# Loading batch 0 in head groups, filling TensorE's early gaps, and placing every step anew in an attention and channel-mix kernel

## The chip, the cores and the metric

The kernel runs on one core of a Trainium2 chip. The metric is device time in microseconds (us) from the start to the end of one execution. The kernel before takes 203.94 us (median of three runs, 203.87 to 204.32).

A core has five engines, each with its own instruction stream that it works off in order: TensorE (PE in the profile; its weight loads are listed as PEld), VectorE (DVE), ScalarE (ACT), GpSimd (POOL) and SyncE (SP). They meet only through semaphores. Transfers between HBM and the on-chip memory are issued by one of the engines and carried out by 16 DMA engines that all queues share.

## The reference

Two layers follow each other. B = 8 batches, H = 8 heads, S = 576 positions, D = 64, M = 32 memory slots; then a channel mix with d_model = 512 and d_ff = 1024.

```python
a = softmax(phi, axis=2)                          # over the 32 slots
k_m = einsum('bhsm,bhsd->bhmd', a, k)
v_m = einsum('bhsm,bhsd->bhmd', a, v)
attn = softmax((1 / sqrt(D)) * q @ k_m.T)         # 576 x 32 per head
x = attn @ v_m                                    # heads side by side: B x S x 512
x_prev = x shifted by one position, zero first
xk = mu_k * x + (1 - mu_k) * x_prev
xr = mu_r * x + (1 - mu_r) * x_prev
k = maximum(xk @ w_k, 0)
v = k * k @ w_v
out = sigmoid(xr @ w_r) * v
```

The inputs q, k, v and phi are float32 (38 MB read from HBM together with the weights), the output is float32; matrix products run in bfloat16.

## The kernel before, in words

**Layout.** A batch has eight heads. They lie in two parity halves of 64 partitions (`ROWS`) and, along the free dimension, in four head pairs (`HH`). A transfer of k, q or v casts float32 to bfloat16 and is issued by GpSimd; phi stays float32. There are two buffers for each of k, v, q and phi, used by even and odd batches in turn, so a load for batch b+2 has to wait until batch b's readers are done. Loads wait in one queue (POOL's), in the order in which they are issued.

**Steps.** Every piece of work is a named step, and `PLAN` is a flat list of the steps in the order in which they are issued. A step issues its instructions to the engines that it uses; since every engine is in order, `PLAN` also fixes the order on each engine. There is no other scheduler. A word is `batch:step`, `cN:f` (one of 8 feature blocks of chunk N of the first mix matmul), `g:t`, `sg:p`, `o:t` (by tiles of 128 tokens), or `p:what` (a load).

The steps of a batch, with their lines before:
- `exp` (L226, ACT) exponentiates phi; `z` (L248, PE) sums it, with a reciprocal on DVE; `kv`, or `k` and `v` singly (L238, PE), contract it with k and v: 72 small matmuls per call.
- `nk`/`ak` normalise k on DVE or ACT, `tk` (L307, PE, copy L312 on DVE) transposes it; `q0`, `q1` (L325, DVE) transpose two head pairs of q each, as soon as q has landed.
- `s` (L340, PE; four exponentials L345 on ACT) makes the scores. It needs `tk` and both q steps.
- The denominator goes either over PE and ACT (`l0`..`l3` L355/L360, `h..z` or `r..z` L365, products `y` or `w` L389 on DVE) or wholly over DVE (`fe`, `fs`, `fo`, `w`: L370 to L389).
- Batches 0 and 1 multiply attention by v with mu already folded in (`nk0`..`nr1` L435, then `mk1`, `mk0`, `mr1`, `mr0`, L294/L452). Batches 2 to 7 make x (`x0`, `x1`: L294, L401 on ACT), the difference (`dd`, DVE) and the mixes (`k0d`, `k2d`, `r0d`, `r2d` on DVE; `r0e`, `r2e` with a product on ACT).

The steps of the mix: `cN:f` is four matmuls (L525), a relu on ACT (L529) and a square on DVE (L533); `g:t` is four matmuls (L548) and an exponential on ACT (L553); `sg:p` finishes the sigmoid for two tiles on ACT (L559, L560); `o:t` is eight matmuls (L574), a product on DVE (L576) and two stores from SP (L510). `a` and `b` mark halves in chunk 0 and in the first four output tiles.

All PSUM tiles come from one pool of eight.

**Batch 0.** Its k, q and v come as two transfers each of 64 partitions (`0a`, `0b`: one parity half with all four head pairs). The first half is used as soon as it is there: `k0c`, `hn0`, `ht0`, `qh0`, `s0` work on one parity, `k1c`, `hn1`, `ht1`, `qh1`, `s1` on the other. `0:mub` broadcasts mu over partitions from a third and fourth small load (`mu_r`). `0:busy6` issues six matmuls of zeros whose result nobody reads. Later loads are issued partly by `p:` words and partly by `b:load`, which issues phi, k, v and q of batch b+2 together.

Of the kernel before, what the change touches and what calls it, by code (L numbers as in the profile page):

```python
# [19 lines left out]
    "0:exp1 0:mub 0:exp0 p:k:0b 0:k0c 0:z 0:hn0 0:k1c p:q:0a 0:ht0 p:q:0b 0:hn1 p:v:0b 0:qh0 0:qh1 p:v:0a 0:s0 0:l1",  # L20
    "0:ht1 0:h1z 0:l0 0:mu 0:s1 0:y1 0:v1c 0:v0c 0:nk1 p:wk:0-4 0:nr0 p:wr:0-4 p:wk:4-8 0:nk0 0:l3 0:h0z 0:y0 0:l2",
    "0:h3z 0:h2z 0:busy6 0:y3 0:y2 0:nr1 0:mr1 0:mk0 g:3 0:mk1 c0:2a 0:mr0 c0:0a p:phi:1 1:exp 7:load p:k:1 c0:4a",
    "c0:1a g:2 c0:0b c0:6a 1:z c0:5a p:q:1 c0:1b 1:k 1:nk sg:1 g:0 6:load 1:q0 1:tk 1:q1 c0:4b c0:5b g:1 c0:7b c0:2b",
    "1:s p:v:1 c0:7a c0:3b c0:3a c0:6b 1:l2 1:v 1:nk1 1:nr1 1:nk0 p:wv:0-2 1:l1 1:l3 1:nr0 1:h2z 1:h1z 1:l0 1:y2 1:y1",
    "1:h3z p:wv:2-4 0:load 1:load 1:y3 1:h0z 1:y0 o:2a o:3a 1:mk1 1:mk0 1:mr0 2:exp c1:5 c1:0 c1:7 1:mr1 c1:3 2:z",
    "c1:1 c1:4 o:3b sg:0 2:kv 2:nk o:2b 2:tk 2:q0 2:q1 c1:2 c1:6 o:1b 2:s 2:nv o:1a 3:exp 2:fe g:5 g:4 2:fs 2:fo 2:w0",
    "3:z sg:2 2:w1 o:0b o:4 o:5 2:x0 3:kv 3:nk g:7 3:nv 3:q0 2:x1 g:6 2:load 3:tk 3:q1 2:dd o:0a sg:3 2:k0d g:8 3:s",
    "4:exp 2:k2d o:6 o:7 3:l1 3:l3 3:l2 2:r0d 3:l0 c2:4 3:r0z 3:w0 3:r1z 3:w1 c2:1 c2:3 3:load c2:0 c2:7 c2:2 4:z",
    "2:r2d 3:x1 4:q0 c2:5 c2:6 3:x0 4:kv 3:dd 4:q1 4:ak 3:k2d g:9 sg:4 o:8 4:tk o:9 3:k0d 4:av 5:exp g:12 g:11 g:10",
    "5:z 4:s 3:r2d 5:kv 3:r0d 4:fe 5:q0 sg:5 c3:2 5:q1 c3:1 c3:7 4:fs 5:av c3:5 g:13 4:fo 5:load 4:load c3:6 4:w0",  # L30
    "7:exp 4:w1 5:ak c3:4 c3:3 o:10 sg:6 o:11 c3:0 7:q1 4:x1 g:14 g:15 7:z 4:x0 sg:7 7:q0 5:tk 4:dd o:12 o:15 6:exp",
    "7:kv 7:ak 5:s 7:av 4:k2d 4:k0d o:14 5:fe 7:tk 4:r2e 6:z o:13 5:fs c4:3 4:r0e 5:fo c4:4 5:w1 c4:5 6:kv 7:s 6:av",
    "6:ak 5:w0 6:q1 6:q0 c4:6 c4:1 g:19 7:fe c4:2 g:16 g:17 5:x0 c4:0 6:tk c4:7 7:fs 5:x1 sg:8 5:dd g:18 sg:9 o:17",
    "5:k0d 5:k2d 6:s o:16 o:19 o:18 5:r2e 5:r0e c5:5 6:fe c5:1 g:21 c5:2 g:20 6:fs c5:0 6:fo sg:10 6:w0 6:w1 c5:3",
    "g:23 c5:4 c5:6 g:22 c5:7 7:fo 6:x1 o:20 7:w0 7:w1 6:x0 sg:11 6:dd o:21 o:22 7:x0 g:25 6:k0d g:24 6:k2d 7:x1",
    "sg:12 7:dd o:23 7:k0d g:26 7:k2d c6:0 6:r0e c6:1 c6:4 6:r2e c6:7 c6:3 c6:5 c6:2 c6:6 c7:4 7:r0e c7:2 c7:7 c7:3",
    "g:27 7:r2e c7:6 c7:0 sg:13 c7:1 o:26 o:25 c7:5 o:27 g:29 o:24 c8:1 c8:4 g:31 g:28 c8:3 sg:14 c8:6 c8:7 g:30 c8:5",
    "o:28 o:29 sg:15 c8:2 o:30 o:31 c8:0 g:33 g:32 sg:16 g:35 g:34 o:33 o:32 sg:17 o:34 o:35",
]

LOADS = {None: ("phi", "k", "v", "q")}
PRE = "k:0a id:"
# [7 lines left out]
def kernel(  # L50
# [94 lines left out]
    def preload(word):  # L145

        what, _, part = word.partition(":")
        if what in weights:
            dst, src = weights[what]
            f0, f1 = (int(x) * 128 for x in part.split("-"))  # L150
            nc.gpsimd.dma_start(out=dst[:, :, f0:f1], in_=src[:, :, f0:f1])
        elif what == "id":
            make_identity(nc, identity)
        else:
            n = int(part[0])
            if what == "phi":
# [19 lines left out]
    sel = const.tile([HH, HH, M], F32, name="sel")  # L176
    nc.vector.tensor_copy(sel, identity[0:HH, 0:HH].unsqueeze(2).to_broadcast([HH, HH, M]))
# [14 lines left out]
    def keep_busy(n):  # L192

        ps = psum.tile([128, CT], F32, name="idle", tag="ps", bufs=8)
        for _ in range(n):
            nc.tensor.matmul(ps.rearrange("p (a b) -> p a b", b=128), lhsT=zeros, rhs=zeros.unsqueeze(1).to_broadcast([128, CT // 128, 128]), start=True, stop=True,  # L196
                             skip_group_check=True)

    def load_mu_b():
        ps = psum.tile([128, 2, 2, D], F32, name="mub", tag="ps", bufs=8)  # L200
        nc.tensor.matmul(ps.rearrange("p w c d -> p (w c d)"), lhsT=sel.rearrange("k g m -> k (g m)"),
                         rhs=mu_r.rearrange("k w c d -> k (w c d)"), start=True, stop=True,
                         skip_group_check=True)
        nc.vector.tensor_copy(mu_m[:, :, 0], ps)
        nc.vector.tensor_scalar(mu_m[:, :, 1], ps, -1.0, 1.0, op0=AL.mult, op1=AL.add)
# [6 lines left out]
    def attention(b):  # L212
# [15 lines left out]
        def ekv(parts, cs=(0, 1)):  # L228

            def go():  # L230
                w = parts.stop - parts.start
                kvps = {c: ps_tile([128, w, D], F32, "kvps") for c in cs}
                for i in range(w):
                    st.setdefault("kv"[parts.start + i], {}).update({c: kvps[c][:, i, :] for c in cs})
                for j in range(NJ):
                    for g in range(HH):
                        for c in cs:
                            nc.tensor.matmul(kvps[c][g * M:(g + 1) * M], lhsT=em[ROWS[c], j, g, :],  # L238
                                             rhs=kv5[ROWS[c], parts, g, j, :],
                                             start=j == 0, stop=j == NJ - 1,  # L240
                                             skip_group_check=True)
            return go
# [54 lines left out]
        def reload():  # L297
            if b + 2 < B:
                load_batch(b + 2)

        def tr_k(cs=(0, 1)):

            def go():
# [8 lines left out]
                nc.vector.tensor_copy(st["kmT"][rows_], ps[rows_])  # L312
# [116 lines left out]

        def norm_mu(w, c):  # L430

            def go():
                if ("vm", w) not in st:
                    st["vm", w] = work.tile([128, 2, 2, D], BF16, name="vm", tag="vm", bufs=2)
                nc.vector.scalar_tensor_tensor(  # L435
                    st["vm", w][:, :, c], in0=st["v"][c].unsqueeze(1).to_broadcast([128, 2, D]),
                    scalar=st["rz"][:, c:c + 1], in1=mu_m[:, w, :, c], op0=AL.mult, op1=AL.mult)
            return go

        def mixed(w, hf):  # L440

            def go():
# [7 lines left out]
                for i in range(ND):  # L450
# [6 lines left out]
                 "z": esum, "nk": norm_k(), "nv": norm_v(), "ak": norm_k(by_act=True), "av": norm_v(True), "tk": tr_k(), "s": scores((0, 1)), "load": reload, "mu": load_mu, "mub": load_mu_b,  # L457
                 "zr": sum_rows}
        steps.update(fe=fold_e, fs=fold_sum, fo=fold_out)
        for i in range(2):  # L460
            steps[f"q{i}"] = turn_q(slice(0, 128), slice(2 * i, 2 * i + 2))
            steps[f"qh{i}"] = turn_q(ROWS[i], slice(0, HH))
            steps[f"k{i}c"] = ekv(slice(0, 1), (i,))
            steps[f"v{i}c"] = ekv(slice(1, 2), (i,))
            steps[f"exp{i}"] = lambda i=i: exp_phi(slice(2 * i, 2 * i + 2))
            steps[f"hn{i}"] = norm_k((i,))
            steps[f"ht{i}"] = tr_k((i,))
            for w in range(2):
                steps[f"n{'kr'[w]}{i}"] = norm_mu(w, i)
# [45 lines left out]
    def keys(c):  # L515
# [3 lines left out]
        def key(fi, lo, hi):  # L519
            def go():  # L520
# [8 lines left out]
                nc.scalar.activation(rl, pk, AF.Relu)  # L529
                cut = min(hi, -(lo + 1) // (2 * S) * (-2 * S))  # L530
                for p0, p1 in ((lo, cut), (cut, hi)) if cut < hi else ((lo, hi),):
                    p = p0 % (2 * S)
                    nc.vector.tensor_mul(sq[:, fi, p:p + p1 - p0], rl[:, p0 - lo:p1 - lo], rl[:, p0 - lo:p1 - lo])  # L533
            return go

        if c == 0:
            return {f"{fi}{'ab'[hf]}": key(fi, sl.start, sl.stop) for fi in range(NF) for hf, sl in enumerate(HALVES)}
        return {str(fi): key(fi, start, end) for fi in range(NF)}
# [92 lines left out]
```

## Time and profile before

| what | value |
|---|---|
| median of the runs | 203.94 us |
| profiled execution: span from first to last instruction | 202.5 us |
| between the two, outside the span | 1.4 us |
| PE busy | 187.8 us (93%) |
| ACT busy | 156.7 us (77%) |
| DVE busy | 147.2 us (73%) |
| POOL busy | 29.3 us (14%) |
| loads through POOL's queue | 20.91 MB written on chip |
| first matmul starts | 5.90 us |
| last matmul ends | 198.8 us |

How to read it: the span is the profiled execution's own time; the runs are timed without the profiler, and the difference is what lies around the span. The second part of the page cuts the span in 40 slices of 5.06 us and gives each engine's busy share in tenths. A row of the groups has the line, the engine, what is written from what, the number of instructions, their busy time and mean length, and then the idle time in front of them with its cause. The DMA issues list the time from issue to landing.

### The profile page before, as it was taken

The page shows a single profiled execution, that of the slowest core. Times are in us where ns is not written, and L with a number is a line of the kernel's source. Part 1 is how long each engine was busy: PE and PEld are TensorE (multiplying, and loading weights), DVE is VectorE, ACT ScalarE, POOL GpSimd, SP SyncE. Part 2 cuts the span into 40 slices and gives each one's busy share as a digit, 9 for nine tenths or more (in the row PEclk, how much of TensorE's full clock was granted, in tenths as well). Part 3 has the DMA queues.
Part 4 walks back from the last instruction along what each step waited for, and adds up shares of the span by engine and source line. Part 5 has one row for each costly group of instructions (what it writes and reads, how often), then busy time and mean ns, then how long its engine had stood idle before and what let it go on. Part 6 is the DMA issues. An engine that isn't in the chain of part 4 may idle for free.

```text
span 202.5 us, 5375 instructions
## 1 busy us (share of the span) xinstructions
PE 187.8 (93%) x2167; PEld 97.2 (48%) x2167; DVE 147.2 (73%) x348; ACT 156.7 (77%) x312; POOL 29.3 (14%) x45
## 2 busy tenths in 40 slices
PE   0649899999999999999999999999999999999992
PEld 0414476646655445544456754444444444444451
DVE  2276646966898989999789979998998845243232
ACT  3135799796858989899896999988899993493670
POOL 7643222212204100036000000000000000000000
PEclk9999999999999999999999999999999999999999
DMA  6999999999999999979999300530242004404425
GB/s 154 156 206 206 267 207 201 263 221 269 224 260 251 245 305 218 276 135 206 258 247 257 95 0 3 122 85 3 55 104 53 0 3 96 112 0 104 107 63 144
DMA packets 24537, 31.29 MB, mean 155 GB/s; under 512 B 1968, under 2 KB 19648, under 8 KB 24512
## 3 DMA queue, kind: packets, MB, share of 16 engines
q0 software_dynamic: 17392, 20.91, 55.5%
q1 hardware_dynamic: 6352, 9.19, 17.4%
q10 hardware_dynamic: 768, 0.85, 1.3%
q8 instruction: 17, 0.28, 0.5%
q14 instruction: 8, 0.07, 0.1%
HBM read 38.28 MB, written 9.44 MB: 236 GB/s over the span
## 4 chain that ended last, share of the span: by engine, by line
PE 90%; DMA 4%; ACT 2%; DVE 1%; POOL 1%; issue 1%; POOLq 0%
PE pk L525 31%; PE pv L574 30%; PE pr L548 16%; DMA q<-in_q_dram 4%; PE kvps L238 3%; PE scps L340 2%; PE mxps L294 2%; PE nops L294 2%; PE zps L355 1%; PE idle L196 1%; PE zps L248 1%; DVE qT L325 1%; POOL kv L111 1%; PE ktps L307 1%; ACT lz L360 0%
## 5 line engine op out<-in xcount | busy, mean ns | idle before, releaser
L525 PE MATMUL pk<-xkT,wk 128*128 128x512 bf16 (+4 forms) x352 | 67.9, 340 | 0.0
L574 PE MATMUL pv<-wv,sq 128*128 128x512 bf16 (+1 forms) x328 | 66.4, 353 | 0.0
L529 ACT ACTIVATE rl<-pk 128x512 bf16<-128x512 f32 (+3 forms) x80 | 41.5, 566 | 13.6 <-PE pk L525 12.7
L525 PEld LDWEIGHTS <-wk 128*128 128x128 bf16 x352 | 32.9, 98 | 28.7 <-issue 0.8
L533 DVE TENSOR_TENSOR sq<-rl 128x512 bf16<-128x512 bf16 (+5 forms) x104 | 31.5, 334 | 19.4 <-ACT rl L529 18.8
L574 PEld LDWEIGHTS <-sq 128*128 128x128 bf16 x328 | 31.1, 98 | 29.7 <-issue 0.8
L548 PE MATMUL pr<-wr,xrT 128*128 128x512 bf16 x144 | 35.4, 379 | 0.8 <-ACT xkT L452 0.8
L576 DVE TENSOR_TENSOR o<-sg,pv 128x512 f32<-128x512 f32 (+1 forms) x41 | 24.5, 616 | 13.3 <-PE pv L574 13.1
L553 ACT ACTIVATE sg<-pr 128x512 f32<-128x512 f32 x36 | 21.4, 610 | 5.9 <-PE pr L548 5.1
L548 PEld LDWEIGHTS <-xrT 128*128 128x128 bf16 x144 | 13.4, 98 | 15.5 <-ACT xkT L452 1.0
L559 ACT ACTIVATE sg<-sg 128x1024 f32<-128x1024 f32 x18 | 19.4, 1079 | 0.2
L560 ACT ACTIVATE sg<-sg 128x1024 f32<-128x1024 f32 x18 | 19.0, 1058 | 0.6
L401 ACT CAST x<-nops 128x320 bf16<-128x320 f32 (+1 forms) x48 | 15.7, 424 | 3.2 <-PE nops L294 3.2
L345 ACT ACTIVATE e<-scps 128x288 bf16<-128x288 f32 x32 | 10.6, 415 | 8.3 <-PE scps L340 8.1
L325 DVE STREAM_TRANSPOSE qT<-q 128x576 uint32<-128x576 uint32 (+1 forms) x16 | 13.3, 839 | 1.2 <-DMA q<-in_q_dram 1.1
L389 DVE TENSOR_TENSOR atn<-e,lz 128x576 bf16<-128x576 bf16 (+2 forms) x20 | 12.1, 634 | 0.9 <-ACT lz L365 0.5
L424 ACT ACTIVATE mu_d<-diff,mu 128x576 bf16<-128x576 bf16 x16 | 11.6, 798 | 0.2 <-DVE xkT L427 0.2
L226 ACT ACTIVATE em<-ph 128x1152 bf16<-128x1152 f32 (+1 forms) x9 | 9.5, 1060 | 2.5 <-DMA ph<-in_phi_dram 2.5
L427 DVE TENSOR_TENSOR xrT<-x,mu_d 128x1152 bf16<-128x1152 bf16 x12 | 9.1, 755 | 3.2 <-ACT mu_d L424 3.0
L426 DVE TENSOR_SCALAR mu_d<-diff,mu 128x576 bf16<-128x576 bf16 x32 | 10.2, 363 | 0.0
L238 PE MATMUL kvps<-kv,em 64*32 64x128 bf16 (+1 forms) x720 | 8.9, 218 | 0.9 <-DMA kv<-in_k_dram 0.9
L108 POOL DMA_DIRECT2D kv<-in_k_dram x7 | 5.2, 746 | 31.3 <-PE kvps L238 26.3
(65 smaller groups left out, 148.1 us busy)
## 6 DMA issues: line engine op xcount, KB each, us to landing
out_dram<-o SPq DMA_DIRECT2D x61, 128.0 KB, 2.4
ph<-in_phi_dram POOLq DMA_DIRECT2D x7, 576.0 KB, 19.1
kv<-in_k_dram POOLq DMA_DIRECT2D x7, 576.0 KB, 18.0
q<-in_q_dram POOLq DMA_DIRECT2D x7, 576.0 KB, 19.8
kv<-in_v_dram POOLq DMA_DIRECT2D x7, 576.0 KB, 21.0
out_dram<-o SPq DMA_DIRECT2D x18, 64.0 KB, 5.9
wk<-in_moe_w_k_dram POOLq DMA_DIRECT2D x2, 512.0 KB, 15.6
wv<-in_moe_w_v_dram POOLq DMA_DIRECT2D x2, 512.0 KB, 20.6
```

The lines of the kernel that those rows point to most:

```text
L238: nc.tensor.matmul(kvps[c][g * M:(g + 1) * M], lhsT=em[ROWS[c], j, g, :], rhs=kv5[ROWS[c], parts, g, j, :], start=j == 0, stop=j == NJ - 1 ...
L325: nc.vector.transpose(dst.bitcast(U32), src.bitcast(U32))
L401: nc.scalar.copy(st["x"][:, i, sl], pss[i])
L525: nc.tensor.matmul(pk[:, p0 - lo:p1 - lo], lhsT=wk_sb[:, di, fi * 128:(fi + 1) * 128], rhs=xk_T[:, di, p0 % RING:p0 % RING + p1 - p0], sta ...
L529: nc.scalar.activation(rl, pk, AF.Relu)
L533: nc.vector.tensor_mul(sq[:, fi, p:p + p1 - p0], rl[:, p0 - lo:p1 - lo], rl[:, p0 - lo:p1 - lo])
L548: nc.tensor.matmul(pr, lhsT=xr_T[:, di, c0:c0 + 128], rhs=wr_sb[:, di, :], start=(di == 0), stop=(di == ND - 1))
L553: nc.scalar.activation(sg[:, t % 2], pr, AF.Exp, scale=-1.0)
L559: nc.scalar.activation(gated[p], gated[p], AF.Ln, bias=1.0)
L560: nc.scalar.activation(gated[p], gated[p], AF.Exp, scale=-1.0)
L574: nc.tensor.matmul(pv[:, cols], lhsT=sq[:, fi, p:p + 128], rhs=wv_sb[:, fi, cols], start=(fi == 0), stop=(fi == NF - 1))
L576: nc.vector.tensor_mul(o[:, cols], gated[t // 2][:, t % 2, cols], pv[:, cols])
```

## The change

Batch 0's transfers are cut by head pairs instead of by parity: `0g` is head pairs 0 and 1, `0h` head pairs 2 and 3, both over all 128 partitions. They are issued in the order k `g`, q `g`, k `h`, q `h`, v `g`, v `h` (before: k a, k b, q a, q b, v b, v a). `kg0`, `kg1`, `vg0`, `vg1` contract one group each into the same PSUM tiles; normalisation, transposition and q's turn then cover all 128 partitions. `nm0` and `nm1` (one for each parity) fold mu in for both mixes in one instruction each. The two `mu_r` loads go; `mub` uses `mu2`, which is loaded anyway, and two matmuls. 36 matmuls of zeros (before: six) stand in seven places ahead of `0:mk1`. 19 relus run on DVE (words with `v`) instead of ACT. `3:r0e` and `3:r2e` take a product from DVE to ACT, `7:r2d` brings one back; `nv`/`av` and `nk`/`ak` change sides in batches 2, 3 and 7. All loads are `p:` words of their own, in another order, and the whole `PLAN` is another one.

```diff
 PLAN = [
-    "0:exp1 0:mub 0:exp0 p:k:0b 0:k0c 0:z 0:hn0 0:k1c p:q:0a 0:ht0 p:q:0b 0:hn1 p:v:0b 0:qh0 0:qh1 p:v:0a 0:s0 0:l1",
-    "0:ht1 0:h1z 0:l0 0:mu 0:s1 0:y1 0:v1c 0:v0c 0:nk1 p:wk:0-4 0:nr0 p:wr:0-4 p:wk:4-8 0:nk0 0:l3 0:h0z 0:y0 0:l2",
-    "0:h3z 0:h2z 0:busy6 0:y3 0:y2 0:nr1 0:mr1 0:mk0 g:3 0:mk1 c0:2a 0:mr0 c0:0a p:phi:1 1:exp 7:load p:k:1 c0:4a",
-    "c0:1a g:2 c0:0b c0:6a 1:z c0:5a p:q:1 c0:1b 1:k 1:nk sg:1 g:0 6:load 1:q0 1:tk 1:q1 c0:4b c0:5b g:1 c0:7b c0:2b",
-    "1:s p:v:1 c0:7a c0:3b c0:3a c0:6b 1:l2 1:v 1:nk1 1:nr1 1:nk0 p:wv:0-2 1:l1 1:l3 1:nr0 1:h2z 1:h1z 1:l0 1:y2 1:y1",
-    "1:h3z p:wv:2-4 0:load 1:load 1:y3 1:h0z 1:y0 o:2a o:3a 1:mk1 1:mk0 1:mr0 2:exp c1:5 c1:0 c1:7 1:mr1 c1:3 2:z",
-    "c1:1 c1:4 o:3b sg:0 2:kv 2:nk o:2b 2:tk 2:q0 2:q1 c1:2 c1:6 o:1b 2:s 2:nv o:1a 3:exp 2:fe g:5 g:4 2:fs 2:fo 2:w0",
-    "3:z sg:2 2:w1 o:0b o:4 o:5 2:x0 3:kv 3:nk g:7 3:nv 3:q0 2:x1 g:6 2:load 3:tk 3:q1 2:dd o:0a sg:3 2:k0d g:8 3:s",
-    "4:exp 2:k2d o:6 o:7 3:l1 3:l3 3:l2 2:r0d 3:l0 c2:4 3:r0z 3:w0 3:r1z 3:w1 c2:1 c2:3 3:load c2:0 c2:7 c2:2 4:z",
-    "2:r2d 3:x1 4:q0 c2:5 c2:6 3:x0 4:kv 3:dd 4:q1 4:ak 3:k2d g:9 sg:4 o:8 4:tk o:9 3:k0d 4:av 5:exp g:12 g:11 g:10",
-    "5:z 4:s 3:r2d 5:kv 3:r0d 4:fe 5:q0 sg:5 c3:2 5:q1 c3:1 c3:7 4:fs 5:av c3:5 g:13 4:fo 5:load 4:load c3:6 4:w0",
...
-    "o:28 o:29 sg:15 c8:2 o:30 o:31 c8:0 g:33 g:32 sg:16 g:35 g:34 o:33 o:32 sg:17 o:34 o:35",
+    "0:busy17 0:exp0 p:q:0g 0:q0 0:mub 0:exp1 0:z 0:kg0 0:busy7_1 p:k:0h 0:kg1 0:busy2_2 0:nk p:q:0h 0:q1 0:tk",
+    "0:busy3_3 0:s0 p:v:0g 0:s1 0:busy2_4 0:l1 0:h1z 0:l3 0:busy2_5 p:v:0h 0:y1 0:vg1 0:h3z 0:y3 0:l0 0:l2 0:vg0",
+    "0:busy3_6 0:nm1 0:nm0 0:h2z 0:y2 0:h0z p:wk:0-4 0:y0 0:mk1 0:mk0 c0:2b 0:mr1 c0:1b p:wk:4-8 c0:5a c0:0av p:phi:1",
+    "c0:4bv c0:5bv 1:exp c0:4a c0:3a 0:mr0 1:z c0:3b c0:2a p:wr:0-4 c0:6b g:3 c0:0b c0:7av g:2 sg:1 0:mu p:k:1 1:k",
+    "1:nk p:q:1 1:q1 1:q0 g:1 g:0 1:tk c0:1av 1:s c0:7bv c0:6a 1:l0 p:wv:0-2 1:h0z o:3a 1:l3 1:l2 1:h2z 1:l1 1:y0",
+    "o:2a 1:h3z 1:y2 p:v:1 1:v 1:nk1 1:nk0 1:nr1 1:y3 1:h1z 1:y1 sg:0 o:0a p:wv:2-4 o:1a 1:mk0 p:phi:2 o:1b 2:exp",
+    "o:3b 1:mk1 1:nr0 o:2b p:v:2 p:k:2 c1:2 c1:5v 1:mr1 c1:7 c1:4 2:z 2:kv 2:nk 1:mr0 p:q:2 2:q0 c1:3 2:av 2:tk 2:q1",
+    "c1:1 c1:0 c1:6v 2:s o:0b 2:fe 2:fs 2:fo 2:w0 p:phi:3 3:exp p:v:3 p:phi:4 g:4 g:6 2:w1 g:5 3:z sg:2 o:4 o:5 4:exp",
+    "2:x1 p:k:3 3:kv 3:nk 4:z 3:av p:q:3 2:x0 3:q1 g:7 3:q0 3:tk g:8 p:k:4 2:dd 2:k0d 3:s 2:k2d sg:3 o:6 3:l0 3:l3",
+    "3:l2 2:r0d 3:l1 3:r0z 3:w0 o:7 3:r1z 3:w1 c2:4 c2:6 p:v:4 p:phi:5 c2:1 5:exp 2:r2d c2:3 c2:0 p:q:4 4:q1 4:kv",
+    "4:av 4:q0 3:x0 c2:2 c2:5 4:ak p:q:5 c2:7 5:z 3:x1 3:dd 3:k2d g:11 g:10 sg:5 4:tk 5:q0 3:k0d 5:q1 g:9 o:11 o:10",
+    "sg:4 o:8 3:r0e 4:s p:k:5 p:phi:6 p:v:5 5:kv 4:fe 4:fs 5:av 5:ak 3:r2e o:9 5:tk c3:7 6:exp c3:0 c3:3 4:fo c3:5",
+    "5:s 5:fe 4:w1 4:w0 g:13 c3:2 c3:4 g:14 5:fs c3:1 p:q:6 4:x1 c3:6 6:z 5:fo 4:x0 4:dd 4:k0d 4:k2d 5:w1 g:15 p:q:7",
+    "sg:7 g:12 sg:6 p:k:7 o:12 o:14 5:w0 p:phi:7 o:15 7:exp p:k:6 c4:5 c4:1 o:13 6:q1 7:z 6:q0 7:q0 4:r2e p:v:7 5:x1",
...
+    "c8:6v g:32 g:33 sg:16 g:28 c7:4v c8:0v sg:14 c8:7v o:28 c8:1 o:29 g:31 g:30 sg:15 o:30 o:33 o:31 g:34 g:35 sg:17",
+    "o:34 o:32 o:35",
 ]
-PRE = "k:0a id:"
+PRE = "k:0g id:"
...
-    mu_r = const.tile([HH, 2, 2, D], F32, name="mu_r")
-    for w, mu in enumerate((moe_mu_k, moe_mu_r)):
-        nc.sync.dma_start(out=mu_r[:, w], in_=mu.rearrange("(h c d) -> h c d", c=2, d=D))
...
+                if part[1:] in ("g", "h"):
+                    gs = slice(0, 2) if part[1] == "g" else slice(2, 4)
+                    nc.gpsimd.dma_start(out=dst[:, gs].rearrange("p h j d -> p h (j d)"), in_=rows(src)[:, gs])
...
-                for j in range(NJ):
-                    for g in range(HH):
+                for j in range(NJ):
+                    for g in gs:
...
+        def norm_both(c):
+            def go():
...
+                nc.vector.scalar_tensor_tensor(
+                    st["vm2"][:, :, :, c].rearrange("p w s d -> p (w s) d"),
+                    in0=st["v"][c].unsqueeze(1).to_broadcast([128, 4, D]),
+                    scalar=st["rz"][:, c:c + 1], in1=mu_m[:, :, :, c].rearrange("p w s d -> p (w s) d"),
+                    op0=AL.mult, op1=AL.mult)
...
-                nc.scalar.activation(rl, pk, AF.Relu)
+                if by_dve:
+                    nc.vector.tensor_scalar_max(rl, pk, 0.0)
+                else:
+                    nc.scalar.activation(rl, pk, AF.Relu)
```

## The prediction

> **What bounds the kernel now.** I read the slices first, to see which engine is full when.
>
> ```profile
> PE   0649899999999999999999999999999999999992
> ...
> DVE  2276646966898989999789979998998845243232
> ACT  3135799796858989899896999988899993493670
> ...
> DMA  6999999999999999979999300530242004404425
> ```
>
> From the fourth slice on TensorE is full, so the time is a front, some 180 us of TensorE work, and a tail. But the DMA row is full as well: from the second slice to the seventeenth, which ends at 86 us, and after one dip again to 111 us. The chain in order of time gives the edges:
>
> ```profile
> 3.13 7.54 DMA q<-in_q_dram
> ...
> 10.70 1.38 DVE qT L325
> ...
> 12.12 0.75 PE scps L340 x13
> ...
> 17.07 2.07 PE idle L196 x6
> 19.14 0.23 PE mxps L294 x4
> ...
> 85.57 0.83 PE kvps L238 x72
> ...
> 198.80 0.42 DVE o L576
> ```
>
> Batch 0's mixes (mxps) start at 19.1 us; from there to 198.8 TensorE is idle only 0.80 us before `g:3` (20.9) and 0.39 us at 38. The tail is one product and stores, 3.7 us.
>
> Then the loads. The issues, each asked for in its own window, give the microseconds to landing; the timeline gives the issue.
>
> ```profile
> 42.89 0.75 POOL L104 DMA_DIRECT2D ph<-in_phi_dram  x1 [2.89 <-ACT em L226]
> ...
> 61.93 0.75 POOL L108 DMA_DIRECT2D kv<-in_v_dram  x1
> ...
> 70.00 0.75 POOL L104 DMA_DIRECT2D ph<-in_phi_dram  x1 [4.79 <-ACT lz L360]
> ```
> ```profile
> ph<-in_phi_dram POOLq DMA_DIRECT2D x1, 576.0 KB, 20.0
> kv<-in_v_dram POOLq DMA_DIRECT2D x1, 576.0 KB, 21.0
> ph<-in_phi_dram POOLq DMA_DIRECT2D x1, 576.0 KB, 17.3
> ```
>
> Phi of batch 4 (phi4) lands at 62.9, v5 at 82.9, phi6 at 87.3, all about 20 us after issue: POOL issues far ahead, and a load lands when all issued before it has gone through. So up to 87 us a load's place in the queue, and not its issue, sets its landing. Batch 5's contraction `5:kv` ran at 85.50 with v5 there since 82.9: it did not wait.
>
> **The change, part by part.** The sum is made against the profiled execution (202.5 us; the median, 203.94, is 1.4 above it, taken as unchanged).
>
> *Front.* The new transfers have the old sizes, so by place the halves land as before: 7.47 (kvps waited for it), 9.00, 10.68 (the chain's 3.13 + 7.54), 12.39, 13.83, 15.39 (POOL's waits for them). The 17 idle matmuls end at 0.93 + 17 x 0.345 = 6.8 (0.345 is the mean of the six at 17.07), ahead of k `g`; at the later rows' 0.215 (`pr`, 0.86 for 4) or double that they end between 4.6 and 8.2, still covered, since k `h` comes only at 10.7. Then `kg1` 0.67 to 11.4, `nk` 0.61 to 12.0, but q `h` lands at 12.4: `q1` 0.77 and, behind it on VectorE, `tk`'s copy 0.25 make 13.4. Scores 0.25 and four exponentials 1.32: 15.0. Eight denominator steps on ScalarE, start to start 0.28 to 0.36: 2.6, with 0.3 for the first sum: 17.9. The last product 0.49: 18.4. So `0:mk1` starts at 18.5 instead of 19.1: 0.6 gained. The other 19 idle matmuls (at most 1.5 us in one place) lie in these waits. The missing `mu_r` loads and the fewer normalisations lie under the same waits: 0. `mub`'s two matmuls (1.19 cold) come before k `h`: 0.
>
> The trace shows the early matmuls at about half rate, though PEclk reads full in every slice: 0.345 against 0.215. *The Trainium skill, "TensorE: Matmul & The Clock Gate", Part 1, says that TensorE starts at half clock and is released after about 3.4 us of sustained matmuls; the early idle matmuls would then run the front's real ones at full clock. By it the scores (0.75 + 0.61 against 0.41 for both) and sums would give an estimated 1 us more, and `0:mk1` would start at 17.5.* The sum goes without that, since the loads below take either.
>
> *Gaps.* `c0:2b` waits for `mk1`'s copies (ACT 0.65, DVE 0.76 for two), with `mk0` (0.41) between: 0.4 of idle instead of 0.80. The 0.39 at 38 goes, because output halves now stand between `1:y1` and `1:mk0`. Gain 0.8 at most.
>
> *Relus.* 19 go from ScalarE (0.48 start to start for 512 columns) to VectorE. No VectorE relu is in the trace. Nearest are its copies of PSUM to bf16 (L452: 0.42 for 256, 0.48 for 320 columns); 0.60 start to start (L576) is the upper end for 512, 0.34 (a square, L533) the lower. I take 0.60: about 10 us more on VectorE, 157 of 202. Its worst pile-up: `5:fo 4:dd 4:k0d 4:k2d 5:w1`, 1.30 + 1.48 + 2 x 1.24 + 0.67 = 5.9 us; the first user, `c4:5`, comes after two `g` and three `o` = 6.9 us of TensorE. Covered by 1.0, so 0; if the cover goes, the excess falls on TensorE.
>
> *Loads, by place in the queue.* Old order from batch 3: phi3 k3 v3 q3 phi4 k4 v4 q4 phi5 k5 v5 q5 phi6; new: phi3 v3 phi4 k3 q3 k4 v4 phi5 q4 q5 k5 phi6 v5. Two places matter.
> - q3 now has phi4 before it: it lands where phi4 did, 62.9. Behind it on VectorE: two turns 0.69 + 0.77, the copy 0.2, so `3:s` starts at 64.6 (old: 64.82); `2:dd` and the mixes queue behind these. TensorE itself would be there at 64.82 - 0.6 - 0.8 + 0.2 (`4:z` comes earlier) = 63.6. It waits 1.0.
> - v5 now has q5 and phi6 before it: it lands where phi6 did, 87.3. TensorE arrives at 64.6 + 20.7 (old distance) - 0.2 + 0.9 (one `g` more ahead, 0.86) = 85.9. Everything behind `5:kv` on TensorE waits: the c3 chunks and, through them, all outputs.
>
> What stores do to v5: o:8 and o:9 went out at 83 to 85, in phi6's last stretch. There the loads' queue (q0) falls from 117.9% of the engines' time (80 to 82 us) to 77.9% (84 to 85) and 23.9% (85 to 86.5), while the stores' (q1) takes 23.3% and 69.1%. New o:11, o:10 and o:8 come at about the same time or later. One tile of stores more or less, 256 KB at the loads' rate (576 KB in 2.8 us, k1 to q1), is 1.3 us: v5 lands between 86.0 and 88.6. I take 87.0, a little below the place's own value, because the stores then rather follow. *The Trainium skill, "DMA: Bandwidth & Descriptors", Queues, rings and completion order, says that each DMA engine takes turns between its queues packet by packet; the shares just given agree with it; by it v5 lands near 86 if the new stores come late, and the time would be 203.5.*
>
> Behind `5:kv` the old order has o:10 and o:11, the new one o:9 and `g:12`: 0.86 less. Old distance from `5:kv` to the last matmul's end: 198.77 - 85.50 = 113.27. New end: 87.0 + 113.27 - 0.86 = 199.4, against 198.77: +0.6. Tail unchanged: after `sg:17` come `o:34 o:32 o:35`, 5.2 us of TensorE over 2.6 us of ScalarE, and the last store issues are the same. 203.94 + 0.6 = **204.5 us**.
>
> **The rivals.**
> - *TensorE paces it (faster).* v5 comes before TensorE asks. The deciding point: if `5:kv` starts before 87.0 - 0.6 = 86.4 the new kernel wins. With only q3 late, the end is 64.6 - 64.82 - 0.2 = -0.4: 203.5. With neither late, -0.6 - 0.8: 202.5. I take 203.1. For it: stores may come late, and the old engines' waits for k, q and phi come to only 4.5 us in all (phi 2.5, q 1.1, k 0.9). Against it: the same bytes stand before v5, and the DMA row has no dip before 86 us. *The clock gate's rule above would add its 1 us only here.*
> - *More waits than these (slower).* VectorE's pile-up outlasts its cover, or v6 is late too: v6 is now the last load. The old last one, q6, was issued at 93.88 and v6 before it landed at 93.14 + 14.7 = 107.8, so by place v6 lands at about 111, and `6:kv` is reached at 87.9 + 23.3 = 111.2. Each adds up to 1.2: 206.
> - *Nothing changes.* The wait at `5:kv` and the gains cancel: 203.9.
>
> **How the numbers follow.** Forecast (paced by v5) 0.52, its own range 203.5 to 205.9 from v5's 86.0 (where TensorE's own 85.9 is the floor) to 88.4; faster rival 0.25; more waits 0.17; cancelling 0.06. A measurement of this kernel tells about 0.2% (0.41 us) from no change. Of the forecast a third lies within 204.35, so same is 0.17 + 0.06 = 0.23; slower 0.35 + 0.17 = 0.52; faster 0.25. The range 202.6 to 206.4 takes in the faster rival's 202.5 nearly and most of the slower one's; about 2 in 10 lie outside.
>
> **What would show it.** Right: a TensorE wait of 0.5 to 2 us before kvps near 86, put down to a DMA of v, and one before scps near 64, put down to VectorE's qT; mxps first at about 18.5; the DMA row full to about 111 without the dip after 86. Wrong: no TensorE gap at 86 (the faster rival), or gaps after 95 before pk, pv or kvps (more waits). The prediction falls if v5 lands before 86.4.

## The result, and the profile after

The changed kernel takes 206.08 us (median of 4 runs, 206.07 to 206.46) beside 203.91 for the kernel before: a ratio of 1.0115, with an interval of 1.0098 to 1.0132. It is slower by 2.2 us; 0.6 was forecast. The profile shown is that of the run of 206.46 us. The medians of the kernel before differ by up to 0.4 us from one chip to the next (203.53 to 203.91 below), so experiments are compared by their ratio to it on the same chip, or within one chip.

The slices of the changed kernel, as they were shown for the kernel before (40 slices, now of 5.12 us):

```profile
PE   8868999898898999999999999999999999999990
...
DVE  2147968775898999999999999979797987762330
ACT  3137869855598999999899988976899926495350
...
DMA  6999999999999999999997300060603162004334
```

TensorE is busy in the first slices now (the idle matmuls), and the DMA row has no dip before its end at about 111 us. The chain in order of time (start, length, what):

```profile
4.02 8.15 DMA q<-in_q_dram
13.72 1.32 ACT e L333 x4
...
43.44 20.67 DMA q<-in_q_dram
64.13 1.44 DVE qT L313 x2
...
87.82 1.19 ACT e L333 x4
...
194.53 5.21 PE pv L587 x32
```

The row at 43.44 is the load of q3, which lands at 43.44 + 20.67 = 64.11: it sets the chain until then. There is no row of v5 near 86, where the forecast had its gate. What TensorE waited for (us in total, times, longest):

```profile
PE kvps L230 <- DMA kv<-in_k_dram: 2.3, 3, 1.2
PE scps L328 <- DVE kmT L300: 1.2, 3, 0.6
...
PE pv L587 <- ACT sg L572: 0.6, 1, 0.6
...
PE scps L328 <- DVE qT L313: 0.4, 1, 0.4
```

By place, those behind batch 0's front are: 0.55 us ahead of `o:0a` at 37.8, 0.77 ahead of `2:kv` at 47.1 (for k2), 0.29 and 0.36 in `2:s` at 52.7 and 53.3 (for q2's turn and the copy behind it), 0.59 ahead of `3:s` at 65.2 (the same for q3). After 66 us TensorE has no idle time of 0.15 us or more up to its last matmul.

The starts of the steps, read from the timelines, for one execution each; the third column is a second profiled execution of the changed kernel, e9 below.

| us | before | after | after, e9 |
|---|---|---|---|
| first scores of batch 0 | 12.12 | 13.20 | 12.85 |
| `2:kv` | 47.49 | 47.84 | 47.42 |
| `2:s` | 51.92 | 53.01 | 52.63 |
| `3:s` | 64.82 | 65.80 | 64.71 |
| `5:kv` | 85.50 | 87.25 | 86.44 |
| last matmul ends | 198.76 | 199.74 | 198.88 |
| last store issue ends | 199.87 | 201.62 | 200.77 |
| last store packet lands | 201.10 | 202.74 | 201.88 |
| last instruction ends | 202.47 | 204.68 | 203.83 |

From `3:s` to the last matmul both kernels need the same: 133.94 us before, 133.94 after (134.17 in e9). So the last matmul is later by what `3:s` is later, 0.98 us in these two executions; e9 shows that one execution scatters by 0.9. Over more executions the difference is about the same: the last matmul ends at 198.76, 198.02 and 198.26 in the three of the old order (the kernel before, e2, e7) and at 199.74, 199.25, 199.11 and 198.88 in four of the new one (the changed kernel, e1, e5, e9), 0.9 later on average. The rest comes behind the last matmul: 3.71 us before, 4.94 after, 4.95 in e9. This 1.23 is the larger part of the loss, and it stands in two places: from the last matmul to the end of the last store issue 1.11 against 1.88, and from the last landing to the end 1.37 against 1.94 (between them the changed kernel is 0.11 shorter).

Here is the end of the kernel before in its timeline (start, length, engine, line, what):

```profile
196.55 3.16 SPq L510 DMA_DIRECT2D out_dram<-o  x4
...
197.10 1.24 DVE L576 TENSOR_TENSOR o<-sg,pv 128x512 f32<-128x512 f32 x2 [1.09 <-PE pv L574]
```

And that of the changed kernel:

```profile
196.29 1.06 ACT L573 ACTIVATE sg<-sg 128x1024 f32<-128x1024 f32 x1
...
197.38 1.34 DVE L589 TENSOR_TENSOR o<-sg,pv 128x512 f32<-128x512 f32 x2 [3.84 <-ACT sg L573]
198.09 2.65 SPq L518 DMA_DIRECT2D out_dram<-o  x4
...
198.90 0.42 DVE L589 TENSOR_TENSOR o<-sg,pv 128x256 f32<-128x256 f32 x1 [0.18 <-PE pv L587]
199.77 0.42 DVE L589 TENSOR_TENSOR o<-sg,pv 128x256 f32<-128x256 f32 x1 [0.45 <-PE pv L587]
```

Before, the products wait for TensorE. After, o:34's product waits 3.84 us for `sg:17` on ScalarE, with o:32's behind it on VectorE. Both come out together at 197.4 to 198.7, and from 198.09 on SyncE issues stores with pauses of 0.2 us at most. (This window ends at 200.5 and counts four issues; the fifth, the last of `o:35`, ran from 200.83 to 201.62, though its product was done at 200.19.)

### The profile page after: what moved, and what is told of

Same layout as the page of the kernel before. It is cut to its first block, busy times and chain, and to the rows that moved or that the text cites. A ratio compares the mean times of both kernels' runs of the same rounds, so it can differ in the third digit from the quotient of the medians.

```text
span 204.7 us, 5403 instructions
## 1 busy us (share of the span) xinstructions
PE 192.6 (94%) x2197; PEld 98.5 (48%) x2197; DVE 155.8 (76%) x362; ACT 152.3 (74%) x295; POOL 30.0 (15%) x45
## 4 chain that ended last, share of the span: by engine, by line
PE 68%; DMA 14%; ACT 10%; DVE 2%; POOL 2%; issue 1%; POOLq 0%; ACTq 0%
PE pk L533 27%; PE pv L587 23%; DMA q<-in_q_dram 14%; PE pr L561 12%; PE kvps L230 2%; ACT e L333 2%; ACT sg L572 2%; PE scps L328 1%; PE nops L286 1%; DVE qT L313 1%; ACT sg L573 1%; PE mxps L286 1%; ACT lz L353 1%; ACT sg L566 1%; POOL kv L148 1%
## 5 line engine op out<-in xcount | busy, mean ns | idle before, releaser
L540 ACT ACTIVATE rl<-pk 128x512 bf16<-128x512 f32 (+3 forms) x61 | 33.8, 570 | 13.8 <-PE pk L533 13.0
L561 PE MATMUL pr<-wr,xrT 128*128 128x512 bf16 x144 | 34.9, 379 | 0.0
L589 DVE TENSOR_TENSOR o<-sg,pv 128x512 f32<-128x512 f32 (+1 forms) x41 | 24.6, 617 | 13.4 <-ACT sg L573 9.6
L313 DVE STREAM_TRANSPOSE qT<-q 128x576 uint32<-128x576 uint32 x16 | 11.9, 763 | 7.8 <-DMA q<-in_q_dram 7.8
L389 ACT CAST x<-nops 128x256 bf16<-128x256 f32 (+1 forms) x48 | 15.8, 435 | 0.9 <-PE nops L286 0.9
L538 DVE TENSOR_SCALAR rl<-pk 128x512 bf16<-128x512 f32 (+3 forms) x19 | 11.3, 594 | 2.5 <-PE pk L533 2.4
L412 ACT ACTIVATE mu_d<-diff,mu 128x576 bf16<-128x576 bf16 x18 | 13.0, 780 | 0.0
L184 PE MATMUL idle<-zeros 128*128 128x512 bf16 x36 | 10.4, 426 | 1.0 <-DVE zeros L115 1.0
L401 DVE TENSOR_TENSOR diff<-x 128x1024 bf16<-128x1024 bf16 (+1 forms) x18 | 8.9, 552 | 2.2 <-ACT x L389 2.2
L230 PE MATMUL kvps<-kv,em 64*32 64x128 bf16 (+1 forms) x720 | 8.2, 210 | 2.3 <-DMA kv<-in_k_dram 2.3
```

The costliest lines, as they stand in the source:

```text
L313: nc.vector.transpose(dst.bitcast(U32), src.bitcast(U32))
L389: nc.scalar.copy(st["x"][:, i, sl], pss[i])
L561: nc.tensor.matmul(pr, lhsT=xr_T[:, di, c0:c0 + 128], rhs=wr_sb[:, di, :], start=(di == 0), stop=(di == ND - 1))
L589: nc.vector.tensor_mul(o[:, cols], gated[t // 2][:, t % 2, cols], pv[:, cols])
```

## The experiments

In these diffs only the words that differ are shown.

**The order of the last outputs, both ways (e1, e2).**

```diff
 changed kernel, e1
-g:34 g:35 sg:17 o:34 o:32 o:35
+g:34 g:35 sg:17 o:32 o:34 o:35
 kernel before, e2
-g:35 g:34 o:33 o:32 sg:17 o:34 o:35
+g:35 g:34 o:33 sg:17 o:34 o:32 o:35
```

> The changed kernel with o:32 and o:34 exchanged at the end, nothing else. Theory A (the order of the last outputs lengthens the tail: o:34's product waits for sg:17 on ScalarE until 197.4, o:32's product stands behind it on VectorE, and both tiles' stores then stand on SyncE ahead of o:35's): the last TensorE matmul stays at 199.7, the last stores are issued about 1.2 us earlier, the tail goes from 5.0 back to 3.7 us, and the time from 206.1 to 204.8. Rival B (the tail is longer for another reason, the stores' own transfers, or ScalarE's late end): the tail stays at 5.0 us and the time at 206.1.

> The kernel before with o:32 moved behind sg:17 and o:34, as the changed kernel has it, nothing else. Theory A: the tail grows by about as much as in the changed kernel, 1.0 to 1.3 us, so 203.9 becomes 204.9 to 205.2. Rival B: the order alone costs nothing, 203.9.

Measured: e1 205.44 us, ratio 1.0094 (1.0076 to 1.0111); e2 204.26 us, ratio 1.0030 (1.0015 to 1.0044); the kernel before 203.70 on this chip. In e1 the last issue ends 1.12 us behind the last matmul, in e2 1.88: the two values of the table, exchanged. The timeline of e1:

```profile
195.82 0.69 DVE L589 TENSOR_TENSOR o<-sg,pv 128x512 f32<-128x512 f32 x1 [2.77 <-PE pv L587]
196.53 3.67 SPq L518 DMA_DIRECT2D out_dram<-o  x5
197.60 1.24 DVE L589 TENSOR_TENSOR o<-sg,pv 128x512 f32<-128x512 f32 x2 [1.09 <-PE pv L587]
```

o:32's product no longer stands behind the wait, and its stores are away before o:35's. Theory A is right in kind, at half the size: the order is worth 0.6 us (0.56 in e2's median), not 1.2. e2's interval is clear of 1; e1's overlaps that of the changed kernel, and there the trace shows the gain: its tail is 4.32 us, beside 4.94. What is left lies behind the last landing (1.99 us in e1, 1.31 in e2), where neither theory had looked.

**The exit (e5).** The trace shows POOL last: in the changed kernel its drain stands 0.44 us behind the instruction ahead of it and takes 0.24; in the kernel before 0.08 and 0.09. Nothing of the program differs there. The transfers of instructions (q14) do. The queues from 200 us on (packets, MB, share), kernel before:

```profile
q10 hardware_dynamic: 169, 0.13, 7.5%
q1 hardware_dynamic: 150, 0.12, 6.5%
```

Changed kernel:

```profile
q1 hardware_dynamic: 322, 0.39, 21.8%
q10 hardware_dynamic: 220, 0.22, 13.4%
q14 instruction: 1, 0.01, 0.3%
```

In the kernel before the last 8 KB on q14 came at 152.7 us; in the changed one they start at 204.7, in the exit. They come too late to be what POOL waited for at 203.5, but they suggest that a block of instructions ends there. POOL has 73 instructions against 79: the loads wait in other places. e5 adds four behind the last load:

```diff
     for _, _, _, step in sorted(todo, key=lambda t: t[0]):
         step()
+    filler = const.tile([1, 4], F32, name="filler")
+    for i in range(4):
+        nc.gpsimd.memset(filler[:, i:i + 1], 0.0)
```

> The changed kernel with four one-element memsets on POOL behind its last load, where POOL has nothing else to do. In the trace of the changed kernel the exit, from the last store's landing to the end, is 1.94 us against 1.37 in the kernel before: POOL, with six instructions fewer than before, stands 0.44 us ahead of its drain, and the last 8 KB of instructions come only at 204.7 us, where the kernel before had them at 152.7. Theory F (the exit is longer because POOL's last instructions are fetched late, which depends on how many instructions POOL has): with four more the drain follows at once, and 206.1 becomes 205.5. Rival G (the exit's length has another cause, such as which engine ends last): 206.1 or a little above.

Measured: 205.28 us, ratio 1.0098 (1.0076 to 1.0121). The drain follows after 0.08 us and takes 0.09; from the last landing to the end it is 1.43 us. So theory F holds for where the time goes, 0.5 us, and for the number of instructions on POOL as its cause: with four instructions more and no other change the exit is short again. The ratio alone, 0.0017 below the changed kernel's, is within its interval; the place in the trace is what shows it. In every kernel here the exit is slow where the last 8 KB come in the exit, and short where they come by 161 us. That a fetch is what POOL waits for is argued from this, not shown.

**The loads (e3, e6).** e3 takes phi4 out of q3's way:

```diff
-p:v:3 p:phi:4 g:4 g:6 2:w1 g:5 3:z sg:2 o:4 o:5 4:exp 2:x1 p:k:3 3:kv 3:nk 4:z 3:av p:q:3
+p:v:3 g:4 g:6 2:w1 g:5 3:z sg:2 o:4 o:5 2:x1 p:k:3 3:kv 3:nk 3:av p:q:3 p:phi:4
...
-3:s
+3:s 4:exp
...
-4:q1
+4:z 4:q1
```

> The changed kernel with phi of batch 4 loaded behind q of batch 3, and its exponentials and their sum (4:exp, 4:z) put behind 3:s, where the kernel before had them. Theory C (the place of q3 in the load queue still sets TensorE's start of 3:s, its last wait): q3 lands about 2 us earlier, the wait of 0.58 us ahead of 3:s goes, 4:z's 0.38 us moves behind it, and with TensorE full from there on the end comes 0.6 us earlier: 205.5. Rival D (the wait is taken up later, or VectorE's and ScalarE's queue holds 3:s just as long): 206.1; and if ScalarE then waits for phi4 at 63 us, up to 1 us more, 207.

Measured: 208.20 us, ratio 1.0231 (1.0212 to 1.0249). q3 landed at 62.1, beside 64.1 in the profile of the result and 63.0 in e9. Its first turn came at 63.16 (e9: 63.04), and `3:s` started at 64.81 without a wait (e9: 64.71). But then ScalarE had the exponentials in its fullest stretch. The timeline of e3:

```profile
74.00 1.17 ACT L216 ACTIVATE em<-ph 128x1152 bf16<-128x1152 f32 x1
...
75.70 0.33 PE L286 MATMUL nops<-atn,vb 32*64 32x320 bf16 x5 [0.75 <-ACT rl L540]
...
77.68 1.95 PE L533 MATMUL pk<-xkT,wk 128*128 128x512 bf16 x8 [0.46 <-DVE rz L243]
```

`5:kv` came at 89.22, and 2 us were lost. This is rival D, at twice its price. The early phi4 does delay q3, but it also lets `4:exp` run ahead of the crowd; the gate cannot be taken away by this exchange. e6 moves v5 alone:

```diff
-p:q:5 c2:7 5:z 3:x1 3:dd 3:k2d g:11 g:10 sg:5 4:tk 5:q0 3:k0d 5:q1 g:9 o:11 o:10 sg:4 o:8 3:r0e 4:s p:k:5 p:phi:6 p:v:5 5:kv
+p:v:5 p:q:5 c2:7 5:z 3:x1 3:dd 3:k2d g:11 g:10 sg:5 4:tk 5:q0 3:k0d 5:q1 g:9 o:11 o:10 sg:4 o:8 3:r0e 4:s p:k:5 p:phi:6 5:kv
```

> The changed kernel with v of batch 5 loaded ahead of q of batch 5, nothing else. The forecast's gate (v5 holds 5:kv at about 87): v5 lands near 79, 5:kv starts when TensorE gets there, 86.2 to 86.8, and the time falls by 0.4 to 1.0 us, to 205.1 to 205.7. Rival H (TensorE gets there at 87.2 anyway, as in the profiled execution of the changed kernel, so v5 is no gate): 206.1; if q5 or phi6, now two places later, hold ScalarE or VectorE, up to 1 us more.

Measured: 205.66 us, ratio 1.0110 (1.0087 to 1.0133). v5 landed at 79.7 (issue plus the profile's time to landing), beside 86.9 in the profile of the result and 86.3 in e9, and nothing waits at `5:kv`:

```profile
85.57 0.48 PE L328 MATMUL scps<-qT,kmT 32*32 32x288 bf16 x32
85.98 0.84 PE L230 MATMUL kvps<-kv,em 64*32 64x128 bf16 x72
```

The last matmul ended at 198.60, in an execution whose batch 0 was 0.5 us late; e5 on the same chip, with the old place of v5, ended at 199.11. The times tell no gain apart from none; e11 below says 0.1. So v5 is a gate of little height: TensorE comes to it within 0.1 to 0.7 us of its landing. e4 shows the gate itself.

**VectorE's relus (e4).**

```diff
-c0:0av c0:4bv c0:5bv c0:7av c0:1av c0:7bv c1:5v c1:6v c5:4v c6:1v c7:1v c7:5v c7:6v c7:4v c8:4v c8:5v c8:6v c8:0v c8:7v
+c0:0a c0:4b c0:5b c0:7a c0:1a c0:7b c1:5 c1:6 c5:4 c6:1 c7:1 c7:5 c7:6 c7:4 c8:4 c8:5 c8:6 c8:0 c8:7
```

> The changed kernel with its 19 VectorE relus back on ScalarE, nothing else. If the relus on VectorE cost nothing (TensorE has no idle time after 66 us, and the three relus before that lie beside other work), the time stays at 206.1 or rises, as ScalarE gets some 10 us more work: 206.0 to 207.0. Rival E (VectorE's 11 us more work delay q's turns and the products, so the relus are part of the loss): 205.0 to 205.6.

Measured: 206.17 us, ratio 1.0132 (1.0113 to 1.0151): the time stays. VectorE fell from 155.8 to 145.6 us busy and ScalarE rose from 152.3 to 160.3, and neither counts. In this execution TensorE was a little earlier, and the timeline shows what the forecast had described:

```profile
85.76 0.48 PE L327 MATMUL scps<-qT,kmT 32*32 32x288 bf16 x32
86.98 0.80 PE L229 MATMUL kvps<-kv,em 64*32 64x128 bf16 x72 [0.74 <-DMA kv<-in_v_dram]
```

The same wait for v5 stands in e1 (0.17 us, `5:kv` at 86.83), e5 (0.36, 86.81) and e9 (0.20, 86.44).

**The idle matmuls (e7, e8, e10).** e7 puts the front block into the kernel before; e8 takes all 36 out of the changed one; e10 cuts them to 128 columns and puts all in front, so that the number of instructions stays.

```diff
 kernel before, e7
-0:exp1 0:mub
+0:busy17 0:exp1 0:mub
 changed kernel, e8
-0:busy17 0:busy7_1 0:busy2_2 0:busy3_3 0:busy2_4 0:busy2_5 0:busy3_6
 changed kernel, e10: as e8, and
+0:busy36x1
```

> The kernel before with the 17 idle matmuls put in front, nothing else: the part alone. If the early idle matmuls release TensorE's clock (full at 3.8 us in the changed kernel, at 18.5 us before) and this shortens the front's scores and sums, batch 0's mixes start 0.3 to 1.0 us earlier and the time falls to 203.0 to 203.6. Rival I (the front is paced by loads, VectorE and ScalarE, or the loads of batches 2 and 3 take the gain back): 203.9.

> The changed kernel without its 36 idle matmuls, nothing else. If the clock's early release matters, the first matmuls run at half rate, batch 0's mixes start 0.5 to 1.5 us later, and the time is 206.5 to 207.5. If the front's waits cover them, or the load gates at 47, 53, 65 and 87 us take the difference: 206.1, and no later start of 5:kv than 87.3.

> The changed kernel with its 36 idle matmuls cut to 128 columns and all put in front, none left between the waits; the number of TensorE's instructions is the same. In e8 TensorE stood 1.65 us at 113 us with nothing to wait for, while a block of its instructions was being fetched. Theory J (that stall came from the moved instruction stream, and the idle matmuls themselves are worth nothing, because TensorE waits for v5 at 86.9 with or without them): no stall at 113, 5:kv at 86.8 to 87.3, the same time as the control within 0.4 us. Rival K (the idle matmuls between the waits are worth the 1.9 us that e8 lost): 1.5 to 2 us above the control.

Measured: e7 203.43 us beside 203.53, ratio 0.9998 (0.9985 to 1.0010): nothing, rival I. The windows of e7 (us, TensorE busy, granted clock, DMA share, GB/s) show one reason:

```profile
5.00:10.00 5.00, 4.59 (x94) 1.00 1.19 190
10.00:15.00 5.00, 2.40 (x37) 0.50 1.20 200
15.00:20.00 5.00, 5.00 (x120) 0.50 1.25 208
20.00:25.00 5.00, 4.89 (x85) 0.97 1.16 265
```

The clock is granted in full at 6.63 us, taken back at 10.05 and granted again at 20.29; in the kernel before it came at 18.5. (The view reads 1.00 ahead of the first grant too, but the idle matmuls come 0.43 us apart up to 6.63 and 0.21 behind it.) At 10.05 TensorE had stood for only 0.2 us of its wait of 1.9 us for batch 0's scores, so the length of that wait is not what took the clock. In the 3.41 us before 10.05 TensorE was busy for 87%, while the changed kernel kept the clock over such a stretch of 60% (7.25 to 10.67 us), with seven idle matmuls in it. What decides is not shown by these runs. What they show is that seventeen matmuls in front did not hold the clock in the kernel before, and that the changed kernel, with 19 more in its later waits, held it from 3.84 to 201.8 us.

e8: 207.82 us, ratio 1.0206 (1.0182 to 1.0230), 1.8 above the changed kernel by the ratios. But it was not late by 87 us: `5:kv` started at 86.90. The loss comes at 113 us:

```profile
111.60 1.54 PE L229 MATMUL kvps<-kv,em 64*32 64x128 bf16 x135
...
114.78 0.28 PE L229 MATMUL kvps<-kv,em 64*32 64x128 bf16 x9 [1.65 <-issue]
```

In the middle of 144 short matmuls TensorE stands 1.65 us and waits for nothing that the profile shows; a transfer of 16 KB of instructions ran from 112.1 to 113.3. That TensorE stood for these instructions is argued from the times, not shown. e10 has no such stall, at 206.63 us, ratio 1.0152 (1.0120 to 1.0184), against 205.97 for e9 on the same chip. Its windows:

```profile
5.00:10.00 5.00, 1.36 (x49) 0.79 1.14 169
10.00:15.00 5.00, 2.18 (x71) 0.50 1.22 207
15.00:20.00 5.00, 2.72 (x83) 0.50 1.20 257
20.00:25.00 5.00, 4.97 (x63) 0.50 1.22 216
```

Here the clock was full from 4.5 to 7.9 us and then at half until 25.0, and `2:kv` started at 50.0 instead of 47.4; by `5:kv`, 87.97 against 86.44, some of that was made up. Theory J is right on the stall: with the instructions' number kept it is gone. On the worth of the fillers it is not settled: 0.7 us by the medians, but e10's runs spread from 205.72 to 207.31 and the two intervals overlap.

**The control and the three edits together (e9, e11).** e9 is the changed kernel again; e11 has the edits of e1, e5 and e6.

> The changed kernel as it is, as the control beside the next two, and a second profiled execution of it. Ratio to the kernel before 1.010 to 1.013; 5:kv at 86.8 to 87.3, waiting for v5 where TensorE comes before 86.8; tail about 5.0 us with the slow exit of 1.9.

> The changed kernel with the three edits together: o:32 ahead of o:34, four memsets on POOL at its end, v5 loaded ahead of q5. If the three are separate costs, they add: 0.6 + 0.57 + 0.2 to 0.5, so 1.4 to 1.7 us below the control, 0.7 to 0.9 above the kernel before on the same chip, or less if batch 0's mixes are not late as in e6; the tail is 3.7 us, as in the kernel before. If they share a cause, less than 1 us below the control.

Measured on one chip: the kernel before 203.62, e9 205.97, ratio 1.0120 (1.0093 to 1.0147), e11 204.82, ratio 1.0058 (1.0037 to 1.0080). The tail of e11 is 3.84 us, near the 3.71 of the kernel before. `5:kv` came at 86.44 in e9, a little ahead of the 86.8 to 87.3 expected. The intervals of e9 and e11 do not overlap. 1.15 us are won, 1.11 of it in the tail by the traces; v5's part is 0.1 (`5:kv` at 86.35), so my sum of 1.4 to 1.7 was too high by that term. 1.2 us stay, nearly all ahead of the last matmul. None of the versions is faster than the kernel before; e11 is the fastest of the complete changed ones.

**The stores (e12).** e12 leaves out the stores of the first four output tiles, so it does not write these outputs.

```diff
-            eng.dma_start(out=dst, in_=o[p:p + n, cols])
+            if t > 3:
+                eng.dma_start(out=dst, in_=o[p:p + n, cols])
```

> The changed kernel with the stores of tiles 0 to 3 (batch 0's outputs, 1 MB) left out, so these outputs are not written; all else as it is. In the changed kernel the stores moved 855 KB between 40 and 52 us against 273 KB in the kernel before, and k2 and q2 landed 0.8 and 1.4 us later. Theory L (early stores slow the loads, and these hold 2:kv, 2:s and 3:s): k2 lands by 46.5 and q2 by 49.2, the waits of 0.5 to 0.8 us ahead of 2:kv and of 0.7 in 2:s go, 3:s starts at 64.0 or earlier, and v5 lands earlier too; the time falls by 0.6 to 1.2 us, to a ratio of 1.006 to 1.009. Rival M (the loads' bytes alone set the landings): the waits stay, ratio 1.011 to 1.013.

The queues from 40 to 52 us (packets, MB, share of 16 engines), q0 the loads' and q1 the stores'. Before:

```profile
q0 software_dynamic: 1926, 2.58, 108.9%
q1 hardware_dynamic: 331, 0.27, 9.1%
```

After:

```profile
q0 software_dynamic: 1594, 2.18, 90.0%
q1 hardware_dynamic: 1046, 0.85, 27.4%
```

e12:

```profile
q0 software_dynamic: 2029, 2.93, 117.5%
```

The load of q3 as the issues list it (issued at 43.24), in e12:

```profile
q<-in_q_dram POOLq DMA_DIRECT2D x1, 576.0 KB, 16.7
```

Measured: 204.21 us, ratio 1.0025 (1.0011 to 1.0039). By issue plus time to landing, k2 lands at 45.8 instead of 47.7, q2 at 48.7 instead of 51.6, q3 at 60.0 instead of 64.1 (63.0 in e9); the waits at 47, 53 and 65 us are gone, `3:s` starts at 62.95 and `5:kv`, without a wait, at 84.46. The timeline at `2:kv`, changed kernel:

```profile
47.84 0.80 PE L230 MATMUL kvps<-kv,em 64*32 64x128 bf16 x72 [0.77 <-DMA kv<-in_k_dram]
```

and e12:

```profile
46.70 0.80 PE L230 MATMUL kvps<-kv,em 64*32 64x128 bf16 x72
```

Theory L holds, and 1.9 us are won where 0.6 to 1.2 were expected. It is an upper bound for the loss: the kernel before pays for these stores too, only later (0.51 MB of stores went out between 52 and 60 us, against 0.04 in the changed kernel). That their early place alone makes the remaining 1.2 us was not tried, since a store cannot be held back without a wait on some engine.

## Why the prediction was right or wrong

The direction was right, and the range held the time; the size was not: 204.5 against 206.1. That the direction came out is for the most part luck: by e11 the gate that the sum rested on is worth 0.1 us, and the loss lies in places that the sum held unchanged or left out. By its own steps:

- *Front.* Forecast: scores at 13.4, batch 0's mixes at 18.5. Seen: 13.20; the first eight mix matmuls at 17.93, the rest at 18.73. Right to 0.2 for the scores and the rest, 0.6 too late for the first eight. The clock rule's sentence had `0:mk1` at 17.5. The clock was full from 3.84 us, 2.85 us behind the first idle matmul; in other executions of the same seventeen it took 2.7 (e4) to 6.0 us (e6). The Trainium skill's "TensorE: Matmul & The Clock Gate", Part 1, has it at about 3.4 us of sustained matmuls. These times lie around that figure and scatter widely. The front gained about 0.6 by the idle matmuls: from the first scores to the first mixes 4.73 us, against 5.31 in e8, without them and with the clock at half up to 23.1 us. The rest of the chain there runs over q's landing, VectorE and ScalarE. (The 0.345 taken for an idle matmul was a mean over both clocks: the starts are 0.40 to 0.43 apart up to 18.5 us, then 0.22.)
- *Gaps.* `c0:2b`'s 0.4 was 0.19. "The 0.39 at 38 goes" was wrong: `o:0a` waits there 0.55 for `sg:0` on ScalarE.
- *Relus.* Forecast 0.60 each and about 10 us, at no cost. Seen 0.594 on average (0.62 the median) and 11.3; e4 shows no cost.
- *q3.* Forecast: it lands at 62.9, `3:s` at 64.6 after a wait of 1.0. Seen: landed at 64.1, the turns at 64.13, `3:s` at 65.80 after 0.59. In six other executions with the same places of phi4 and q3 (e1, e4, e5, e6, e9, e11) q3 landed at 62.8 to 63.2 and `3:s` came at 64.5 to 65.0, after a wait of 0.2 at most. So the landing is right but for the profile of the result, where it was 1.2 late, and 64.6 for `3:s` came out by luck; what failed is "TensorE itself would be there at 63.6". It was there at 65.2, and in e9 at 64.6, after waits of 1.4 us (1.3 in e9) for k2 and q2 that the sum did not have: "Two places matter" left out batch 2, whose loads keep their places but for v2 and k2 exchanged, though 0.58 MB more of stores now ran beside them. I had priced stores only where v5 lands (e12 shows what they cost here).
- *v5, the named gate.* Forecast: landing between 86.0 and 88.6, taken as 87.0; `5:kv` waits there, TensorE arriving at 85.9 (its own sum gives 86.0). Seen: landed at 86.9 in the profile of the result and at 86.3 to 86.9 in e1, e4, e5 and e9; there `5:kv` came after a wait, at 86.44 to 86.98, TensorE arriving at 86.2 to 86.7. The gate is there; in the profiled execution of the result TensorE came to it last, at 87.25. I had used the packet-by-packet turns of the Trainium skill's "DMA: Bandwidth & Descriptors", Queues, rings and completion order, for a landing near 86. The landings lie between that and the 87.0, nearer to the 87.0 in four of the five, and the 203.5 that I drew from it would not follow in any case, since TensorE itself was late. (What the forecast calls phi6 in the old queue is phi7, since `5:load` stands ahead of `4:load`; it has the same size and the sum is not touched.)
- *From `5:kv` to the last matmul.* Forecast 113.27 - 0.86 = 112.41; seen 112.49. The last matmul at 199.4; seen 199.74 and, in e9, 198.88.
- *Tail.* This is the step that failed by most: "Tail unchanged: ... the last store issues are the same". I compared TensorE's time with ScalarE's, 5.2 over 2.6 us, and did not follow o:34's product, which waits for `sg:17` with o:32's behind it on VectorE, to the stores on SyncE. The tail is 1.23 us longer: 0.6 from this order (e1 and e2), 0.5 to 0.6 from POOL's exit (e5), which no row of the kernel before foretold.
- *The test that I set.* "No TensorE gap at 86 (the faster rival)" would have read the profile of the result as a win. It was none, because the time lay in front of the gate and behind the last matmul.

The rivals: the faster one, no wait for v5, is what e6 makes, and it is not faster: without the gate the ratio is still 1.0110. "More waits than these" was the nearest in time, 206, but not in place: neither VectorE's pile-up nor v6 (landed at 109.6, no wait at `6:kv`) did it.

## What to carry to other kernels

Follow the last outputs instruction by instruction, from the product over its engine's order to the store queue: a product that waits for a late operand holds the ones behind it, and their stores then come ahead of the last ones. When outputs move earlier, ask which loads they will run beside; here leaving out 1 MB of early stores brought a load forward by 3 to 4 us (q3, e12), and `3:s` and `5:kv` behind it came 1.8 to 2.9 us earlier. A gate that TensorE reaches about when it lands shows in one execution and not in the next, so compare starts of steps over several executions before a wait is named the bound.

## What the runs showed of the hardware

- *In these kernels the length of the exit goes with POOL's number of instructions.* With 73 (changed kernel, e1, e4, e6, e8, e9, e10, e12) the drain comes 0.42 to 0.44 us behind the instruction ahead of it and takes 0.23 to 0.24; with 75 (e3), 77 (e5, e11) or 79 (before, e2, e7) it comes after 0.08 to 0.09 and takes 0.09 to 0.10. The Trainium skill's "Runtime: NRT & Kernel Launch", Instruction fetch mechanics, says that the cost of crossing a block of instructions is mostly hidden. If a fetch is what POOL waits for here, which is not shown, up to 0.6 us were not hidden, nor the 1.65 us in e8.
- *The granted clock held for whole multiples of 3.41 us.* Its stretches in the traces are 3.41 (e10), 10.24 (e7), 17.07 (e10), 180.9 (e7, e8) and 197.97 us (changed kernel, e5), all whole multiples of 3.413. The Trainium skill's "TensorE: Matmul & The Clock Gate", Part 1, gives a free-running window of this length; the traces agree. Once lost, the full clock stayed away for 10.24 us (e7) and 17.07 us (e10).
- *Behind 195 us a store issue on SyncE took 0.47 to 0.80 us*, and 0.79 for each of the last two of the changed kernel; its five in a row took 3.53 us with the pauses between them (198.09 to 201.62).
